# Row tiles 0 and 1 of a fused prologue in smaller parts, row tile 1's transposes later

## The chip, the cores and the metric

The kernel runs on one core of one Trainium2 chip. The metric is the device time of one execution in microseconds (us). A profile's span, from the first to the last instruction of the profiled execution, is about 1.8 us shorter than that execution's time.

## The reference, cut to what matters

The program normalises x (2048 x 640), runs attention over the last 512 cached positions on it with 32 heads, and multiplies the result with a gate that comes from a SwiGLU network on the same normalised x. Only the start of the network matters here: the first product that needs the normalised x.

```
xn = _layernorm(x, axis=-1)                  # 2048 x 640
s  = attention(xn, k_cache, v_cache, wq, wo)
h  = _silu(xn @ w_gate) * (xn @ w_up)        # the part at the start of the kernel
g  = _silu(h @ w_down)
return x + s * g
```

## The kernel before

The kernel does the network first. The first 512 rows are four row tiles of 128 rows. For each of them VectorE takes the statistics (two `bn_stats` on 320 columns each, one `bn_aggr`), ScalarE the square root, VectorE the reciprocal and the normalised rows `xn`. PE (TensorE, the matmul engine) transposes `xn` in five chunks of 128 columns into two tiles in PSUM, the memory that it writes its results to, and copies bring the chunks to `xnT`. Then PE multiplies: 30 matmuls for each row tile (five chunks, six PSUM banks: gate and up for three blocks of the hidden dimension). The work of row tile t+1 stands inside the matmuls of row tile t, at matmul 24 of 30:

```python
PARTS = (slice(0, 2), slice(2, NC))          # chunks 0-1, chunks 2-4
...
def ready(t):
    xn, rows = xns.pop(t), slice(t * P, (t + 1) * P)
    for tp, cs in zip(tps, PARTS):           # five transposes, two PSUM tiles
        for k, c in enumerate(range(cs.start, cs.stop)):
            nc.tensor.transpose(tp[:, k, :], xn[:, c * P : (c + 1) * P], ident[:])
    for tp, cs in zip(tps, PARTS):           # two copies
        part = tp[:, 0 : cs.stop - cs.start, :]
        if t == 3 and cs.stop == NC:
            nc.vector.tensor_copy(out=xnT[:, cs, rows], in_=part)
        else:
            nc.scalar.copy(xnT[:, cs, rows], part)
...
for k, (f, s, cs) in enumerate(order):
    if k == len(order) * 4 // 5 and t < 3:   # 24 of 30
        ...                                  # ln_apply(t + 1), and statistics of a later tile
        ready(t + 1)
        ...
    hidden_mm(first[f][s][:, rows], s, f, rows, cs)
```

Before all this PE runs 15 matmuls on zeros (`keep_warm`), while x and the weights are being loaded.

The softmax here doesn't subtract the row's maximum and nothing guards it: scores larger than these inputs give would overflow.

## Time and profile before

| | before |
|---|---|
| time, median of the first 3 runs | 922.87 us (922.42 to 922.88) |
| span of the profile | 920.7 us |
| PE busy | 914.6 us, 99% |
| first matmul of row tile 0, 1, 2, 3 | 6.54, 8.61, 10.68, 12.75 us |
| first matmul on 512 columns, after row tile 3 | 14.47 us |

The views are read thus. A timeline row gives the start, the length, the engine (DVE is VectorE, ACT is ScalarE), the line, the operation, its output and inputs, the shapes and the count; in brackets is the idle time before it and what ended it. Rows of one kind are merged, and their length then runs from the first start to the last end. Matmuls are pipelined: one of 128 columns lasts 0.22 us from start to end, and the next one starts 0.0556 us after it. PE's number of instructions in the page of before is 16 short, as some matmul records are missing from that trace.

### The profile page before, as it was taken

To read this page: it belongs to the slowest core of one execution; us is meant where nothing else is said; L and a number is where in the kernel's file an instruction comes from. 1 tells how busy PE (TensorE), PEld (TensorE's weight loads), DVE (VectorE), ACT (ScalarE), POOL (GpSimd) and SP (SyncE) were. 2 spreads that over 40 slices of the span, in tenths; PEclk is the share of its full clock that TensorE was granted. 3 is DMA by queue.
4 is the path that set the end of the run, shared out by engine and by line. 5 is a ranking of instruction groups with operands and counts; after the bars stand their busy time and mean duration, and the time that the engine had idled before them with its cause. 6 is when DMAs were issued, how large, how long until landed. Compare 5 with 4: busy or idle time off the path is not lost.

```text
span 920.7 us, 25767 instructions
## 1 busy us (share of the span) xinstructions
PE 914.6 (99%) x11086; PEld 625.9 (68%) x11102; DVE 575.8 (63%) x847; ACT 474.6 (52%) x850; POOL 101.9 (11%) x390
## 2 busy tenths in 40 slices
PE   9999999999999999999999999999999999999998
PEld 5455556575858585868686767676777777676666
DVE  6343331467676767676766667676767676767656
ACT  4222222556464646565556565655555555556461
POOL 0000000000000000000000000000000000002978
PEclk9999999999999999999999999999999999999999
DMA  9330510045644444435536262635271717163524
GB/s 308 64 75 18 110 35 1 1 78 89 92 74 85 82 83 83 79 87 70 97 62 104 60 108 53 113 48 119 44 122 36 130 37 126 31 129 86 130 62 142
DMA packets 243762, 77.18 MB, mean 84 GB/s; under 512 B 224576, under 2 KB 243648, under 8 KB 243648
## 3 DMA queue, kind: packets, MB, share of 16 engines
q1 hardware_dynamic: 243216, 75.14, 41.9%
q8 instruction: 87, 1.43, 0.7%
q10 hardware_dynamic: 432, 0.39, 0.2%
q14 instruction: 27, 0.22, 0.1%
HBM read 39.45 MB, written 2.62 MB: 46 GB/s over the span
## 4 chain that ended last, share of the span: by engine, by line
PE 98%; POOL 0%; DMA 0%; DVE 0%; issue 0%; POOLq 0%; ACT 0%; DVEq 0%
PE mm L440 22%; PE sc L576 19%; PE sc L454 18%; PE mm L479 16%; PE sc L277 11%; PE mm L299 6%; PE sc L548 2%; PE mm L531 2%; POOL ob L636 0%; PE gu L277 0%; PE mm L548 0%; PE mm L312 0%; DMA x_t<-in_A_x_dram 0%; PE sc L479 0%; PE sc L531 0%
## 5 line engine op out<-in xcount | busy, mean ns | idle before, releaser
L458 ACT ACTIVATE p_t<-sc 128x1024 bf16<-128x1024 f32 x254 | 253.0, 1023 | 128.2 <-PE sc L454 128.2
L445 DVE TENSOR_REDUCE qT<-mm 128x512 bf16<-128x1024 f32 x189 | 231.1, 1223 | 95.3 <-PE mm L440 92.8
L509 ACT ACTIVATE O_b<-mm,r 128x192 bf16<-128x192 f32 x486 | 165.0, 422 | 180.8 <-issue 156.3
L440 PE MATMUL mm<-xnT,wq_p 64*128 64x512 bf16 x1890 | 240.2, 376 | 0.0
L601 DVE TENSOR_TENSOR sacc<-sacc,sc 128x640 f32<-128x640 f32 x200 | 164.2, 821 | 87.0 <-PE sc L576 87.0
L576 PE MATMUL sc<-wo_p,OT_b 64*128 64x320 bf16 x2592 | 217.3, 296 | 0.0
L454 PE MATMUL sc<-qT,khat 64*128 64x512 bf16 x1524 | 198.2, 376 | 0.0
L479 PE MATMUL mm<-V_p,p_t 64*128 64x193 bf16 x3520 | 186.4, 242 | 0.0
L479 PEld LDWEIGHTS <-p_t 64*128 64x128 bf16 x3584 | 162.9, 93 | 12.1
L440 PEld LDWEIGHTS <-wq_p 64*128 64x128 bf16 x1890 | 105.7, 94 | 93.4 <-issue 0.5
L576 PEld LDWEIGHTS <-OT_b 64*128 64x128 bf16 x2592 | 140.4, 94 | 21.4
L454 PEld LDWEIGHTS <-khat 64*128 64x128 bf16 x1536 | 85.9, 94 | 79.8
L564 POOL MEMSET turn_t<- 128x1 f32 x328 | 32.5, 99 | 691.9 <-PE mm L479 469.7
L285 DVE TENSOR_TENSOR hT<-sc,sg 128x512 bf16<-128x512 f32 x46 | 31.7, 691 | 83.7 <-ACT sg L284 83.7
L284 ACT ACTIVATE sg<-sc 128x512 bf16<-128x512 f32 x46 | 27.3, 597 | 73.4 <-PE sc L277 71.9
L277 PE MATMUL sc<-xnT,wg_sb 128*128 128x512 bf16 (+1 forms) x248 | 59.5, 353 | 0.7
L277 PE MATMUL sc<-xnT,wu_sb 128*128 128x512 bf16 (+1 forms) x259 | 60.2, 354 | 0.1
L299 PE MATMUL mm<-wd_sb,hT 128*128 128x320 bf16 x384 | 56.6, 299 | 0.0
L498 DVE RECIPROCAL r<-mm 128x4 f32<-128x4 f32 x124 | 22.6, 182 | 46.9 <-PE mm L479 36.1
L299 PEld LDWEIGHTS <-hT 128*128 128x128 bf16 x384 | 37.6, 98 | 18.9
L277 PEld LDWEIGHTS <-wu_sb 128*128 128x128 bf16 x285 | 27.1, 98 | 26.9 <-issue 0.2
L277 PEld LDWEIGHTS <-wg_sb 128*128 128x128 bf16 x285 | 27.1, 98 | 22.7
(69 smaller groups left out, 374.9 us busy)
## 6 DMA issues: line engine op xcount, KB each, us to landing
wo_p<-in_A_wo_dram SPq DMA_DIRECT2D x16, 480.0 KB, 4.4
K_p<-in_A_k_cache_dram SPq DMA_DIRECT2D x32, 192.0 KB, 3.3
V_p<-in_A_v_cache_dram SPq DMA_DIRECT2D x32, 192.0 KB, 3.0
wq_p<-in_A_wq_dram SPq DMA_DIRECT2D x64, 80.0 KB, 3.0
wq_p<-in_A_wq_dram SPq DMA_DIRECT2D x16, 160.0 KB, 3.4
x_r<-in_A_x_dram SPq DMA_DIRECT2D x16, 160.0 KB, 4.7
x_t<-in_A_x_dram SPq DMA_DIRECT2D x14, 160.0 KB, 3.0
OT_b<-O_b SPq DMA_TRANSPOSE x124, 3.0
```

The source lines that it names most:

```text
L277: nc.tensor.matmul(out, w_sb[:, c, f * P : (f + 1) * P], xnT[:, c, qc], start=(c == 0), stop=(c == NC - 1),)
L285: nc.vector.tensor_tensor(hTs[b][:, f, :], u, sg[:], ALU.mult)
L299: nc.tensor.matmul(dn[:, 0:HD], hTs[b][:, f, ti * P : (ti + 1) * P], wd_sb[:, f, cols], start=(f == 0), stop=(f == NF - 1),)
L440: nc.tensor.matmul(q_ps[:, h, :], pairs[pr]["wq"][r, c, j * P : (j + 1) * P], xnT[r, c, b * 512 : (b + 1) * 512], start=(c == 0), stop=(c ...
L445: nc.vector.reduce_sum(qTs[i][:, j, :], q_ps[:, :, :].rearrange("p h n -> p n h"), axis=AX.X)
L454: nc.tensor.matmul(sc[:, h, :], khat[r, j, ks], qT[r, j, :], start=(j == 0), stop=(j == 2))
L458: nc.scalar.activation(p_t[:, :, :], sc[:, :, :], ACT.Exp, scale=scale)
L479: m = nc.tensor.matmul(acc[:, k, h * 256 : h * 256 + Dh + 1], Ps[i][kc][r, h, qt * P : (qt + 1) * P], V_p[r, kc, h, 0 : Dh + 1], start=(p ...
L509: nc.scalar.activation(O_b[:, qt, h, :], a_k[:, h, 0:Dh], ACT.Copy, scale=r[:, k, h, :])
L564: st["turn"] = nc.gpsimd.memset(turn_t[:], 0.0)
L576: m = nc.tensor.matmul(ps[:, n, 0:HD], OTs[i][r, 3 * qt + j, :], pairs[i // NB]["wo"][r, j, n * HD : (n + 1) * HD], start=(turn == 0 and j ...
L601: nc.vector.tensor_tensor(s_t, s_t, sc[:, :, 0:HD], ALU.add)
```

## The change

The intent: the first product can start earlier if row tile 0's first chunk is ready sooner (parts of 1, 2 and 2 chunks), and VectorE takes the last copy of row tile 0 so that ScalarE isn't in the way. Row tile 1 is normalised in two parts, and its transposes move behind row tile 0's matmuls: two of them at matmul 28, three after matmul 30.

```diff
-        def ready(t):
-            xn, rows = xns.pop(t), slice(t * P, (t + 1) * P)
-            ...                                   # both parts, as above
+        PARTS = {0: (slice(0, 1), slice(1, 3), slice(3, NC)), 1: (slice(0, 2), slice(2, NC))}
+        COLS = {t: [slice(cs.start * P, cs.stop * P) for cs in parts] for t, parts in PARTS.items()}
+
+        def ready(t, n):
+            cs, rows = PARTS[min(t, 1)][n], slice(t * P, (t + 1) * P)
+            tp = tps[n % 2][:, 0 : cs.stop - cs.start, :]
+            for k, c in enumerate(range(cs.start, cs.stop)):
+                nc.tensor.transpose(tp[:, k, :], xns[t][:, c * P : (c + 1) * P], ident[:])
+            if (t, n) in ((0, 2), (3, 1)):
+                nc.vector.tensor_copy(out=xnT[:, cs, rows], in_=tp)
+            else:
+                nc.scalar.copy(xnT[:, cs, rows], tp)
...
-        ln_stats(1, lambda: ln_apply(0, (slice(0, 2 * P), slice(2 * P, D))))
-        ready(0)
+        ln_stats(1, lambda: ln_apply(0, COLS[0]))
+        for n in range(3):
+            ready(0, n)
...
-                if k == len(order) * 4 // 5 and t < 3:
+                if t == 0 and k == 28:
+                    ln_apply(1, COLS[1])
+                    ready(1, 0)
+                elif t in (1, 2) and k == 24:
...
+            if t == 0:
+                ready(1, 1)
+                ln_stats(2)
+                ln_sqrt(2)
```

More of the change, by code (lines that the diff above doesn't have):

```diff
@@ L215 @@
         psum1 = early.enter_context(tc.tile_pool(name="psum1", bufs=1, space=bass.MemoryType.PSUM))
-        PARTS = (slice(0, 2), slice(2, NC))
         tps = [psum1.tile([P, 8, P], bf, name="tp", tag="tp%d" % n) for n in range(2)]
@@ L318 @@
         hTs[0] = ffh.tile([P, NF, 512], bf, name="hT")
-        def ready(t):
-            xn, rows = xns.pop(t), slice(t * P, (t + 1) * P)
-            for tp, cs in zip(tps, PARTS):
-                for k, c in enumerate(range(cs.start, cs.stop)):
-                    nc.tensor.transpose(tp[:, k, :], xn[:, c * P : (c + 1) * P], ident[:])
-            for tp, cs in zip(tps, PARTS):
-                part = tp[:, 0 : cs.stop - cs.start, :]
-                if t == 3 and cs.stop == NC:
-                    nc.vector.tensor_copy(out=xnT[:, cs, rows], in_=part)
-                else:
-                    nc.scalar.copy(xnT[:, cs, rows], part)
+        PARTS = {0: (slice(0, 1), slice(1, 3), slice(3, NC)), 1: (slice(0, 2), slice(2, NC))}
[9 more added lines that the diff above has]
+                nc.scalar.copy(xnT[:, cs, rows], tp)
         ln_stats(0)
         ln_sqrt(0)
-        ln_stats(1, lambda: ln_apply(0, (slice(0, 2 * P), slice(2 * P, D))))
-        ready(0)
+        ln_stats(1, lambda: ln_apply(0, COLS[0]))
+        for n in range(3):
+            ready(0, n)
         ln_sqrt(1)
@@ L354 @@
                     else:
-                        ln_apply(t + 1)
-                    ready(t + 1)
-                    if t == 0:
-                        ln_stats(2)
-                    if t < 2:
-                        ln_sqrt(t + 2)
+                        ln_apply(3)
+                    for n in range(2):
+                        ready(t + 1, n)
+                    if t == 1:
+                        ln_sqrt(3)
                     else:
```

## The prediction

> **What bounds the kernel now.** I read the page first, then the view of waits of the PE, then the timelines of PE, ScalarE and VectorE between 3.5 and 14 us. On the page, the busy line and the chain that ended last:
>
> ```profile
> PE 914.6 (99%) x11086; PEld 625.9 (68%) x11102; DVE 575.8 (63%) x847; ACT 474.6 (52%) x850; POOL 101.9 (11%) x390
> ...
> PE 98%; POOL 0%; DMA 0%; DVE 0%; issue 0%; POOLq 0%; ACT 0%; DVEq 0%
> ```
>
> TensorE sets the end from start to finish. The view of waits for PE has two rows only, both in the first 6 us:
>
> ```profile
> PE gu L225 <- DVE zero_t L174: 1.2, 1, 1.2
> PE tp L326 <- DVE xn L262: 0.2, 1, 0.2
> ```
>
> The stage table says the same: 332.00 us busy of 332.00 between 168 and 500 us, 27.04 of 27.20 between 12.8 and 40 us. After about 13 us nothing can absorb a delay of PE and nothing can profit from an idle engine, so the change is worth exactly what it does to the moment when PE starts on row tile 3, and no more. The change touches only the prologue, where row tiles 0 to 3 are normalised (VectorE), transposed (PE, L326), copied from PSUM (ScalarE, L332) and multiplied (PE, L277).
>
> The timeline there, in which the PE rows give issue times 0.055 us apart and each row's own length overlaps the next:
>
> ```profile
> 5.39 0.64 DVE L262 TENSOR_SCALAR xn<-x_t,mv,rstd 128x256 bf16<-128x256 bf16 x2
> 5.79 0.63 PE L326 MATMUL tp<-ident,xn 128*128 128x128 bf16 x5 [0.19 <-DVE xn L262]
> 6.11 0.82 ACT L332 COPY xnT<-tp 128x256 bf16<-128x256 bf16 x2 [0.96 <-PE tp L326]
> 6.54 0.22 PE L277 MATMUL sc<-xnT,wg_sb 128*128 128x128 bf16 x1
> ...
> 7.88 0.44 PE L326 MATMUL tp<-ident,xn 128*128 128x128 bf16 x5
> 8.19 0.75 ACT L332 COPY xnT<-tp 128x256 bf16<-128x256 bf16 x2 [1.05 <-PE tp L326]
> 8.43 0.22 PE L277 MATMUL gu<-xnT,wu_sb 128*128 128x128 bf16 x1
> 8.61 0.22 PE L277 MATMUL sc<-xnT,wg_sb 128*128 128x128 bf16 x1
> ```
>
> From the first transpose (5.79) to the first matmul of row tile 3 (12.75 in the same view) are 6.96 us; the 20 transposes and 90 matmuls between need 110 x 0.0556 = 6.12. So 0.84 us are holes: 0.18 inside row tile 0's transposes (the third waits for the second part of xn), 0.29 before its first matmul (6.25 to 6.54), and 0.12 before the first matmul of each of row tiles 1, 2 and 3 (8.49 to 8.61, for example). That 0.84 is all there is to win.
>
> A transpose-to-matmul latency follows: row tile 1's first transpose is at 7.88, its copy starts at 8.19 and its first matmul at 8.61, that is 0.73 us. Row tiles 2 and 3 show the same (9.95 to 10.68, 12.02 to 12.75). In that time the kernel has 5 transposes and 6 matmuls to issue, 11 x 0.0556 = 0.61; the missing 0.12 is the hole.
>
> The VectorE timeline is nearly full in this stage:
>
> ```profile
> 6.46 0.21 DVE L241 BATCH_NORM_AGGREGATE mv<-stats 128x2 f32<-128x12 f32 x1
> 7.16 0.16 DVE L260 RECIPROCAL rstd<-rstd 128x1 f32<-128x1 f32 x1 [0.49 <-ACT rstd L251]
> 7.36 0.45 DVE L262 TENSOR_SCALAR xn<-x_t,mv,rstd 128x640 bf16<-128x640 bf16 x1
> 7.72 0.88 DVE L238 BATCH_NORM_STATS2 stats<-x_t 128x6 f32<-128x320 bf16 x2
> 8.63 0.21 DVE L241 BATCH_NORM_AGGREGATE mv<-stats 128x2 f32<-128x12 f32 x1
> 8.76 0.44 DVE L238 BATCH_NORM_STATS2 stats<-x_t 128x6 f32<-128x320 bf16 x1
> 9.21 0.16 DVE L260 RECIPROCAL rstd<-rstd 128x1 f32<-128x1 f32 x1
> 9.40 0.45 DVE L262 TENSOR_SCALAR xn<-x_t,mv,rstd 128x640 bf16<-128x640 bf16 x1
> ```
>
> Row tile 2's xn ends at 9.85; with the 0.05 that a hand-over to PE takes (5.74 to 5.79 for row tile 0) it is ready at 9.90, and PE transposes it at 9.95. So VectorE is only 0.05 us ahead of PE there. From 7.36 to 9.40 it runs without a break.
>
> **What the Trainium skill says.** "TensorE: Matmul & The Clock Gate", Part 2 (Step-by-step): weight loads may be pulled ahead, but "The MATMULs themselves stay in program order". The trace agrees: the transposes and L277 appear in program order, and a stuck transpose holds what follows. The same page (Single matmul latency, Back-to-back issue gap) gives (398 + N)/2.4 = 219 ns and about 56 ns for N = 128; the trace has 219 ns and 0.0556 us. "ScalarE: Activation LUTs", What ACT_TABLE_LOAD costs, gives 0.833 ns per element and a fixed part; the trace's copies take 372 ns for 256 columns and 484 for 384, so 0.875 ns per column, and I use those: 260 ns for 128 columns. "Perfetto Trace Analysis", Optimizing Scalar/DVE Operations: VectorE pays a fixed overhead per instruction (some 60 ns on SBUF, and about twice that in the profile), yet breaking an instruction up may let work finish sooner where it causes bubbles. The trace has a larger price: TENSOR_SCALAR on 256, 384 and 640 columns takes 346, 373 and 446 ns, and the next start follows after 0.26, 0.29 and 0.36 us, so nearly 0.2 us of each is fixed.
>
> **The change part by part.** The order of instructions that the compiler leaves: PE issues all five transposes of row tile 0 (1, 2, 2) before the first matmul, and the third pair waits for ScalarE's copy of part 0, because it reuses its PSUM tile. Row tile 1's transposes move from position 24 of row tile 0's 30 matmuls to position 28 (two chunks), then 2 matmuls, then three chunks.
>
> *Row tile 0.* xn by parts: 128 columns at 5.39, length about 0.32 (346 less 27 for 128 columns), the next starts at 5.62, the third at 5.88. First transpose 5.76; ends 5.99; copy of part 0 at 6.02, ends 6.28. Part 1: xn ends 5.97, transposes 6.02 and 6.08, copy 6.33 to 6.70. Part 2: xn ends 6.23, the PSUM tile is free at 6.28 + 0.06 = 6.34, transposes 6.34 and 6.40. First matmul 6.45, against 6.54: **0.09 us won**. Chunk 1 is needed at 6.45 + 6 x 0.0556 = 6.79 and is there at 6.76. VectorE's copy of part 2 comes behind bn_stats and bn_aggr at about 6.8, ends near 7.1, and is needed at 6.45 + 15 x 0.0556 = 7.28: no wait.
>
> *Row tile 1.* VectorE: the three pieces cost 0.23 + 0.26 + 0.26 = 0.75 against 0.55, so bn_stats starts at 6.14 in place of 5.94; bn_aggr ends 6.87. Before, the square root was held back by ScalarE's copies to 6.83; now it starts at 6.90, so 0.07 later. Reciprocal 7.23, xn part 0 at 7.43, ready for PE at 7.83. PE comes to position 28 at 6.45 + 1.56 = 8.01, so xn isn't waited for; part 1 (7.69 to 8.07) is there too. But from 8.01 the first matmul of row tile 1 still needs the latency of 0.73, so 8.74, and PE has only 2 transposes, 2 matmuls and 3 transposes to put in between: 7 x 0.0556 = 0.39. The hole grows from 0.12 to 0.34. Row tile 1 starts at 8.74 against 8.61: the 0.09 has become **0.13 lost**.
>
> *Row tile 2.* xn of row tile 1 in two parts costs VectorE 0.26 + 0.29 = 0.55 against 0.36, so 0.19; with the 0.07 all that follows is about 0.27 later: row tile 2's xn at 9.67 to 10.12, ready 10.17. PE arrives at its transposes at 8.74 + 24 x 0.0556 = 10.07, so it now waits 0.10. The transposes start 10.17 against 9.95: **0.22 lost**. Code from here on is unchanged: first matmul of row tile 2 at 10.90.
>
> *Row tile 3.* The square root waits for ScalarE's copies, which are 0.22 later with the transposes; xn ready at about 12.16, PE arrives at 12.23: no new wait. First matmul 12.97 against 12.75. The sum is +0.22 us, and it goes through to the end: 922.87 + 0.22 = 923.1.
>
> **The rivals.** First, a gain: the author's intent. If row tile 1's first copy began before 8.1 us, or row tile 2's xn came in time, the 0.09 would stay, and one of the holes could close: 922.5 to 922.8. For it: the earlier first matmul is solid. Against it: the 0.73 latency appears three times alike, and 7 slots can't cover it. Second, VectorE as the bound: if a piece costs more than I read, or its PSUM copy delays the reciprocal, row tiles 2 and 3 both wait for xn and the loss is 0.3 to 0.5: 923.2 to 923.4. For it: the slack of 0.05 before. Against it: bn_aggr's square root gives the copy 0.3 us of idle VectorE to hide in. Third, weights: an earlier first matmul might wait for a DMA. The loads of the first two chunks are issued at 0.72 and 1.23 and take 3.4 and 4.0 us, so they land by 5.3, and those of the rest (1.74 and 2.24, 4.3 and 4.8 us) by 7.1, needed at 7.1 and 7.6. Close for one, but hidden: 0 to 0.1.
>
> **Range and chances.** The whole stage that is touched holds 0.84 us of holes, and no path adds over 1 us; 2% would be 18 us. So neither side of 2% is reachable by this change, and only a disturbed run could show it. The effect I expect, 0.22, is less than the spread of the three runs before (922.42 to 922.88, 0.46). The range is the effect of -0.3 to +0.5 with that spread: 922.4 to 923.6. Faster 0.01, same 0.98, slower 0.01.
>
> **What would show it.** Right: first L277 matmul near 6.45; row tile 1's first transpose near 8.01; a hole of about 0.3 before row tile 1's first matmul (8.74); PE waiting about 0.1 for VectorE's xn at 10.1; first matmul of row tile 3 near 12.97; everything after shifted by the same amount. Wrong: a first matmul after 6.54 (the PSUM reuse costs more), no hole before row tile 1, no wait for xn at row tile 2, or a start of row tile 3 at or before 12.75. Any difference that arises after 14 us would mean that I missed a coupling.

## The result, and the profile after

| | before | after |
|---|---|---|
| time, median of 6 runs each | 922.69 us (922.42 to 922.88) | 922.95 us (922.62 to 923.37) |
| ratio | | 1.0003, 95% interval 0.999 to 1.0016 |
| span of the profile | 920.7 us | 920.9 us |
| first matmul of row tile 0, 1, 2, 3 | 6.54, 8.61, 10.68, 12.75 us | 6.49, 8.79, 10.89, 12.96 us |
| first matmul on 512 columns | 14.47 us | 14.67 us |

A ratio here is the mean time of one kernel's fast runs over that of the other's of the same rounds, so it isn't quite the ratio of the medians. The page after, busy times and the chain that ended last:

```profile
PE 915.7 (99%) x11102; PEld 626.1 (68%) x11102; DVE 576.5 (63%) x850; ACT 474.5 (52%) x850; POOL 101.9 (11%) x390
...
PE 99%; POOL 0%; issue 0%; DVE 0%; POOLq 0%; ACT 0%; DVEq 0%
```

PE still sets the end. VectorE has three instructions more (850 for 847): one more piece of row tile 0, one more of row tile 1, one copy. ScalarE has the same number, as it gained a small copy and gave one away. The view of waits of PE lists:

```profile
PE gu L224 <- DVE zero_t L174: 1.2, 1, 1.2
PE sc L276 <- ACT xnT L332: 0.2, 1, 0.2
```

A wait for ScalarE's copy (L332) is new in the list. That the wait for `xn` of row tile 0 has gone is not the change's doing: in this profile the last warming matmuls took 0.31 us each and their lengths cover it; in the second profile of the same kernel (after_again, below) it is listed again with 0.2 us. PE's timeline shows the new wait, at row tile 1:

```profile
8.00 0.22 PE L276 MATMUL sc<-xnT,wu_sb 128*128 128x128 bf16 x1
8.06 0.28 PE L328 MATMUL tp<-ident,xn 128*128 128x128 bf16 x2
8.17 0.22 PE L276 MATMUL sc<-xnT,wu_sb 128*128 128x128 bf16 x1
8.22 0.22 PE L276 MATMUL gu<-xnT,wu_sb 128*128 128x128 bf16 x1
8.28 0.33 PE L328 MATMUL tp<-ident,xn 128*128 128x128 bf16 x3
8.79 0.22 PE L276 MATMUL sc<-xnT,wg_sb 128*128 128x128 bf16 x1 [0.18 <-ACT xnT L332]
```

From the first transpose (8.06) to the first matmul of row tile 1 (8.79) are 0.73 us, as before. But only seven instructions are issued in that time, the first transpose among them, so PE has issued the last of them at 8.39 and waits to 8.79 for its turn; in issue time the hole is 8.79 - 8.45 = 0.34 us. The brackets show 0.18, because the pipelined lengths run on to 8.61. VectorE's timeline, row tile 1 and 2:

```profile
7.20 0.16 DVE L259 RECIPROCAL rstd<-rstd 128x1 f32<-128x1 f32 x1
7.40 0.64 DVE L261 TENSOR_SCALAR xn<-x_t,mv,rstd 128x256 bf16<-128x256 bf16 x2
7.96 0.88 DVE L237 BATCH_NORM_STATS2 stats<-x_t 128x6 f32<-128x320 bf16 x2
8.87 0.21 DVE L240 BATCH_NORM_AGGREGATE mv<-stats 128x2 f32<-128x12 f32 x1
8.99 0.44 DVE L237 BATCH_NORM_STATS2 stats<-x_t 128x6 f32<-128x320 bf16 x1
9.44 0.16 DVE L259 RECIPROCAL rstd<-rstd 128x1 f32<-128x1 f32 x1
9.64 0.45 DVE L261 TENSOR_SCALAR xn<-x_t,mv,rstd 128x640 bf16<-128x640 bf16 x1
```

The reciprocal comes 0.04 us later than before (7.16 there), the next `bn_stats` 0.24 later (7.72 there), and row tile 2's `xn` 0.24 later (9.40 there).

**Where the 0.2 us is.** It arises before the first 512-column matmul, and nowhere else. The span from that matmul to the end is 920.7 - 14.47 = 906.23 us before and 920.9 - 14.67 = 906.23 after. Over all twelve profiles it lies between 906.17 and 906.34. So the prologue can be compared alone, and far more sharply than the times can. As x arrives a little earlier or later from run to run (VectorE's first `bn_stats` starts between 3.52 and 3.95 us), the experiments are measured from that `bn_stats`. That gives, for the first 512-column matmul, 10.77 us before (14.47 - 3.70) and 10.99 after (14.67 - 3.68): a loss of 0.22.

### The profile page after: what moved, and what is told of

Its sections match the earlier page's. It is cut to its first block, busy times and chain, and to the rows that moved or that the text cites. A ratio compares the mean times of both kernels' runs of the same rounds, so it can differ in the third digit from the quotient of the medians.

```text
span 920.9 us, 25788 instructions
## 1 busy us (share of the span) xinstructions
PE 915.7 (99%) x11102; PEld 626.1 (68%) x11102; DVE 576.5 (63%) x850; ACT 474.5 (52%) x850; POOL 101.9 (11%) x390
## 4 chain that ended last, share of the span: by engine, by line
PE 99%; POOL 0%; issue 0%; DVE 0%; POOLq 0%; ACT 0%; DVEq 0%
PE mm L447 22%; PE sc L583 19%; PE sc L461 18%; PE mm L486 16%; PE sc L276 11%; PE mm L298 6%; PE sc L555 2%; PE mm L538 2%; PE gu L224 1%; POOL ob L643 0%; PE gu L276 0%; PE mm L555 0%; PE mm L311 0%; PE sc L538 0%; PE sc L486 0%
```

## The experiments

All kernels gave correct results. All numbers in the table are us from VectorE's first `bn_stats`, out of the timelines of PE and VectorE, except for the last two columns: the median time, and that of before in the same rounds. "Slow clock" is explained under the table; in after the clock came up only during the transposes, in the others before the first one or at it.

| kernel | row tile 0 | 1 | 2 | 3 | first 512 | time | before |
|---|---|---|---|---|---|---|---|
| before | 2.84 | 4.91 | 6.98 | 9.05 | 10.77 | | |
| before_again (slow clock) | 2.94 | 5.22 | 7.29 | 9.37 | 11.08 | 922.63 | 922.70 |
| after (clock up in the transposes) | 2.81 | 5.11 | 7.21 | 9.28 | 10.99 | 922.95 | 922.69 |
| after_again | 2.76 | 5.05 | 7.22 | 9.29 | 11.00 | 922.92 | 922.70 |
| rt0_parts_only | 2.76 | 4.98 | 7.05 | 9.12 | 10.84 | 922.50 | 922.70 |
| rt1_parts_only | 2.84 | 5.14 | 7.21 | 9.28 | 10.99 | 922.65 | 922.70 |
| pos24_two_pieces | 2.76 | 4.88 | 7.21 | 9.28 | 11.00 | 922.86 | 922.51 |
| pos28_one_piece | 2.75 | 5.05 | 7.12 | 9.19 | 10.91 | 922.77 | 922.51 |
| earlier_transposes | 2.84 | 4.92 | 6.96 | 8.93 | 10.72 | 922.49 | 922.51 |
| earlier_stats | 2.84 | 4.92 | 6.88 | 8.84 | 10.63 | 922.59 | 922.51 |
| earlier_stats_pairs (slow clock) | 2.95 | 5.14 | 7.11 | 9.06 | 10.74 | 922.50 | 922.54 |
| earlier_stats_pairs_again | 2.85 | 4.99 | 6.95 | 8.91 | 10.59 | 922.22 | 922.59 |

Every ratio's interval contains 1, so the times decide none of these; the profiles do.

**The two kernels again, unchanged.**

> The kernel before, unchanged, as a second profile and a null for the times. Measured from VectorE's first bn_stats, the first matmul of row tiles 0, 1, 2, 3 came at 2.84, 4.91, 6.98, 9.05 us in the first profile. If these are set by the order of instructions alone, this run repeats them within 0.03 us, and the time within 0.3 us of its partner. If the clock of the PE array at the start (how long the warming matmuls run slow) moves them, they differ by 0.05 us or more between two profiles of the same kernel, and the loss of 0.23 us in the changed kernel would be in doubt.

> The changed kernel, unchanged, a second profile. From the first bn_stats: 2.81, 5.11, 7.21, 9.28 us for the first matmul of row tiles 0 to 3 in its first profile, so 0.23 us later than before at row tile 3. In that profile the last warming matmuls and the first transpose were still slow (the first transpose 0.29 us against 0.23). If the clock was unlucky, row tile 0 comes 0.04 to 0.07 earlier now (2.74 to 2.77) and all later tiles with it; the loss at row tile 3 would be 0.16 to 0.23. Time 0.2 to 0.3 us longer than its partner.

The changed kernel repeated itself within 0.01 us at row tile 3, this time with the clock up before the first transpose. Row tiles 0 and 1 came 0.05 and 0.06 earlier than in its first profile, as expected; row tiles 2 and 3 did not, against the expectation, because PE then stood 0.07 us before row tile 2's transposes (9.86 to 9.99 us, less one issue), until VectorE's `xn` was there:

```profile
9.86 0.22 PE L276 MATMUL gu<-xnT,wu_sb 128*128 128x128 bf16 x1
9.99 0.45 PE L328 MATMUL tp<-ident,xn 128*128 128x128 bf16 x5
```

The kernel before did not repeat itself: it came 0.32 us later at row tile 3. Its PE timeline:

```profile
5.47 0.42 PE L225 MATMUL gu<-zero_t 128*128 128x128 bf16 x2
5.79 0.79 PE L326 MATMUL tp<-ident,xn 128*128 128x128 bf16 x5
6.64 0.27 PE L277 MATMUL sc<-xnT,wg_sb 128*128 128x128 bf16 x1
6.70 0.31 PE L277 MATMUL sc<-xnT,wu_sb 128*128 128x128 bf16 x1
6.81 0.31 PE L277 MATMUL sc<-xnT,wg_sb 128*128 128x128 bf16 x1
6.92 0.31 PE L277 MATMUL sc<-xnT,wu_sb 128*128 128x128 bf16 x1
```

These matmuls take 0.31 us for 0.22 and follow one another after 0.11 us in place of 0.0556. The Trainium skill, "TensorE: Matmul & The Clock Gate", Part 1 (The HAM clock gate), says that the array starts at half its clock, is released after a window of activity of some 3.4 us, and that the window runs freely, so that the moment differs from run to run. The trace agrees in the spacing (0.11 us against the page's 107 ns at half clock). In this profile the release came only after row tile 0's first matmuls; in the first profile of before it came before the transposes (the warming matmuls follow one another after 0.06 us from 5.21 us on). The clock that the windows view reports stood at 1.00 in both, so it doesn't show this; the durations do. The late clock cost 0.10 us up to the first matmul and 0.21 more up to row tile 1's; from there on the two profiles of before make the same steps (2.07, 2.08 and 1.71 us, against 2.07, 2.07 and 1.72). For the comparison it means that only profiles with the same clock at the transposes may be set side by side, and I could compare the two slow ones (11.08 and 10.74) only with each other. By this rule the pair for the change is before and after_again: 10.77 and 11.00, a loss of 0.23; before with an early clock was profiled once. The changed kernel was never profiled with a clock as late as in before_again, so its loss there is not shown.

**One half of the change at a time.**

```diff
# rt0_parts_only, against the changed kernel
-                if t == 0 and k == 28:
-                    ln_apply(1, COLS[1])
-                    ready(1, 0)
+                if t == 0 and k == 24:
+                    ln_apply(1)
+                    for n in range(2):
+                        ready(1, n)
+                    ln_stats(2)
+                    ln_sqrt(2)
...
-            if t == 0:
-                ready(1, 1)
-                ln_stats(2)
-                ln_sqrt(2)
```

> Row tile 0 in three parts, row tile 1 as before (one normalisation, five transposes at matmul 24). My theory (the loss is made at row tile 1, by its transposes at position 28): row tile 0 at 2.78 to 2.81, row tile 1 at 4.95, row tile 2 at 7.01, row tile 3 at 9.08, so a loss of 0.03 and no gain, because VectorE's xn of row tile 1 sets row tile 1. Rival (VectorE's three pieces and its PSUM copy make the loss): row tile 3 at 9.2 or later.

```diff
# rt1_parts_only, against the changed kernel
-        PARTS = {0: (slice(0, 1), slice(1, 3), slice(3, NC)), 1: ...}
+        PARTS = {0: (slice(0, 2), slice(2, NC)), 1: ...}
-            if (t, n) in ((0, 2), (3, 1)):
+            if (t, n) == (3, 1):
-        for n in range(3):
+        for n in range(2):
             ready(0, n)
```

> Row tile 0 as before, row tile 1 in two parts at matmul 28 and 30. My theory: row tile 0 at 2.84, row tile 1 at 5.13, row tile 2 at 7.19, row tile 3 at 9.26, the whole loss of about 0.21 us with this part alone, and no wait for xn before row tile 2's transposes. Rival (VectorE's work for row tile 0 makes the loss): row tile 3 at 9.05 to 9.10.

Row tile 1's half alone makes the whole loss (first 512 at 10.99, as with both), all of it in the hole before row tile 1 (5.14 for 4.91), and PE doesn't wait for `xn` before row tile 2, as expected. Row tile 0's half alone wins 0.08 us at its own first matmul and has lost 0.07 by row tile 1, a little more than the 0.03 that I had expected; its row tile 3, at 9.12, lies between my 9.08 and the rival's 9.2. Its timeline shows why nothing is left of the win:

```profile
7.68 0.22 PE L276 MATMUL gu<-xnT,wu_sb 128*128 128x128 bf16 x1
7.87 0.45 PE L328 MATMUL tp<-ident,xn 128*128 128x128 bf16 x5
```

PE comes to row tile 1's transposes 0.13 us too soon (7.74, one issue after 7.68) and stands until VectorE has delivered `xn`, which with three pieces for row tile 0 comes 0.07 us later after the first `bn_stats` than before (3.73 for 3.66). The PE that starts earlier has nothing to do earlier.

**Position and pieces.** Row tile 1's half has two parts again: where its transposes stand (24 or 28), and whether VectorE writes `xn` in one piece or two. With row tile 0 in three parts, four combinations were run; they aren't quite a square, as pos24_two_pieces moves two of the five transposes back to 24 and leaves three behind 30, while rt0_parts_only has all five at 24.

```diff
# pos24_two_pieces, against the changed kernel
-                if t == 0 and k == 28:
+                if t == 0 and k == 24:
# pos28_one_piece, against the changed kernel
-                    ln_apply(1, COLS[1])
+                    ln_apply(1)
```

> The changed kernel with row tile 1's first two transposes back at matmul 24 (its other three stay behind matmul 30). All from VectorE's first bn_stats, for a profile with the clock up before the first transpose. Theory (two limits of nearly the same length, the latency from transposes to matmuls and VectorE's chain): the hole before row tile 1 shrinks to 0.12, so row tile 1 at 4.86 in place of 5.05; but VectorE hasn't become faster, so PE now waits about 0.25 us for xn before row tile 2's transposes, and row tile 2 comes at 7.20, row tile 3 at 9.26: the loss stays at about 0.21. Rival (position 28 alone is the cause): row tile 1 at 4.86, no wait for xn, row tile 3 at 9.0 to 9.07.

> The changed kernel with row tile 1 normalised by one instruction again (its transposes and copies stay in two parts at matmul 28 and 30). Theory: row tile 1 at 5.05 as in the changed kernel (latency), VectorE 0.19 earlier afterwards, so no wait for xn before row tile 2; row tile 2 at 7.12, row tile 3 at 9.18: loss 0.13 in place of 0.23. Rival (VectorE's pieces don't matter): row tile 3 stays at 9.28. Other rival (VectorE's pieces are all of it): row tile 3 at 9.05.

| first 512, against 10.77 of before | `xn` in one piece | `xn` in two pieces |
|---|---|---|
| transposes at 24 | +0.07 (rt0_parts_only) | +0.23 (pos24_two_pieces) |
| transposes at 28 | +0.14 (pos28_one_piece) | +0.22, +0.23 (after, after_again) |

Row tile 0's three parts are in every cell, +0.07 by themselves. Beside that the position alone costs 0.07 more and the two pieces alone 0.16 more, and both together cost no more than the two pieces do. In pos24_two_pieces the hole before row tile 1 is back to its old size (row tile 1 at 4.88), and PE waits one step later instead:

```profile
9.92 0.22 PE L276 MATMUL gu<-xnT,wu_sb 128*128 128x128 bf16 x1
10.22 0.45 PE L328 MATMUL tp<-ident,xn 128*128 128x128 bf16 x5
```

The gap from 9.92 to 10.22 is one issue (0.06) and a wait of 0.24 us for row tile 2's `xn`, which VectorE wrote at 9.72 to 10.17. The three transposes left behind matmul 30 don't set this: VectorE ran without a break from row tile 1's first piece (7.49) to row tile 2's reciprocal (9.52), and the square root that the reciprocal needs was done at 9.49. So two limits of almost the same length stand beside each other: PE's latency from transposes to matmuls, and VectorE's chain. The rival "the position alone" has fallen (row tile 3 at 9.28, not 9.07), and so has "the pieces alone" (9.19 with one piece, not 9.05; 0.07 of that is row tile 0's half, which has 9.12 by itself).

**A version that starts row tile 3 sooner.** If this holds, it helps to put the transposes earlier and to shorten VectorE's chain. All three kernels start from the kernel before.

```diff
# earlier_transposes, against the kernel before
-                if k == len(order) * 4 // 5 and t < 3:
+                if k == 22 and t < 3:
...                 # for t == 1: ln_sqrt(3) is issued between the two copies of ready(2)
# earlier_stats, in addition
+        load_x(2)                        # was two lines further down
         load_first(slice(2, NC))
...
         ready(0)
         ln_sqrt(1)
+        st2 = [ln_stats_halves(2)]       # first bn_stats of row tile 2, in VectorE's idle time
...                 # its second bn_stats, bn_aggr and ln_sqrt(2) between the two copies of ready(1)
# earlier_stats_pairs, in addition
-                order = [(*fs, range(NC)) for fs in banks]
+                order = [(f, s, [c]) for f in range(3) for c in range(NC) for s in range(2)]
...
-                if t == 3 and s == 1:
+                if t == 3 and s == 1 and NC - 1 in cs:
```

> The kernel before with the transposes of row tiles 1 to 3 at matmul 22 in place of 24 (two more matmuls to cover the latency) and the square root of row tile 3 put between ScalarE's two copies of row tile 2. Theory: row tile 1 at 4.89 (PE waits for xn), row tile 2 at 6.93 (waits for xn), row tile 3 at 8.88 without a hole, so 0.17 us won over before's 9.05. Rival (the hole returns elsewhere, as ScalarE's second copy is later): row tile 3 at 9.05 or later. In the time 0.2 us is near the noise; 922.5.

> As earlier_transposes, and VectorE's chain shortened: x of row tile 2 is loaded before the weights of chunks 2 to 4, the first bn_stats of row tile 2 runs in VectorE's idle time before row tile 1's reciprocal, and its square root stands between ScalarE's two copies of row tile 1. Theory: row tile 1 at 4.89, row tile 2 at 6.84, row tile 3 at 8.79, holes only before row tile 1: 0.26 us won. Rival: the weights of chunks 2 to 4 land about 0.4 us later and PE waits for them in row tile 0, up to 0.2, so nothing is won. Time 922.3 to 922.5 if the theory holds.

Both went the expected way at row tile 3's first matmul (8.93 and 8.84, expected 8.88 and 8.79), but at the first 512-column matmul only 0.05 and 0.14 us were left of 0.12 and 0.21. PE's timeline of earlier_transposes, row tile 3's first two groups of five matmuls:

```profile
12.61 0.56 PE L277 MATMUL sc<-xnT,wg_sb 128*128 128x128 bf16 x5
13.00 0.44 PE L277 MATMUL sc<-xnT,wu_sb 128*128 128x128 bf16 x5
```

The first group takes 0.39 us to the next (12.61 to 13.00) where five matmuls need 0.28; before took 0.33 (12.75 to 13.08). In this row tile the order is bank by bank, so chunk 2 is wanted 0.11 us after the first matmul, and VectorE's copy of chunks 2 to 4 (12.42 to 12.78 in its timeline) isn't done. Hence the third kernel.

> As earlier_stats, and row tile 3's matmuls in another order: for each pair of gate and up bank, chunk by chunk, so that chunk 2 is needed after 4 matmuls in place of 2. In earlier_stats row tile 3's first group took 0.08 us longer than elsewhere, waiting for VectorE's copy of chunks 2 to 4. Measure: the first matmul on 512 columns after row tile 3, from VectorE's first bn_stats: 10.77 before, 11.00 in the changed kernel, 10.63 in earlier_stats. Theory: 10.55, with the clock up before the first transpose; the rest of the span from there stays at 906.2. Rival: another copy or the SiLU table is waited for, and it stays at 10.63. In the time 0.2 us under before, which five rounds may not resolve beside the spread of about 1 us.

> The same kernel as earlier_stats_pairs, because its profile fell on a start with slow transposes and slow first matmuls (10.74 us from the first bn_stats to the first 512-column matmul, the clock up only at about 7.1 us). If the clock comes up before the first transpose this time: 10.55. If it is late again: 10.7 to 10.8, to be compared with 11.08 of the second profile of before, which had the same late clock.

The first profile of this kernel fell on a late clock (10.74, against 11.08 of before with a late clock); the second one, with the clock up at the first transpose, gave 10.59, so 0.18 us less than before. That it missed 10.55 has a reason that the rival of earlier_stats had named, a late load of weights. In row tile 0 PE stood 0.17 us (7.60 to 7.83, less one issue) for the up weights of chunks 2 to 4, and row tile 1 came at 4.99 in place of 4.92. The view of waits lists it for the weight loads (PEld), not for PE:

```profile
7.60 0.22 PE L288 MATMUL gu<-xnT,wg_sb 128*128 128x128 bf16 x1
7.83 0.23 PE L288 MATMUL sc<-xnT,wu_sb 128*128 128x128 bf16 x1
...
PEld L288 <- DMA wu_sb<-in_B_w_up_dram: 0.2, 1, 0.2
```

So moving the load of row tile 2's x forward is not free: in earlier_stats, where x came 0.31 us later (first `bn_stats` at 3.95), the wait didn't show.

In the second set of times its median was 922.22 us against 922.59 (ratio 0.9995, interval 0.9981 to 1.0008); in the first one 922.50 against 922.54. So it beats both kernels in the profile; the times of the second set lean the same way and don't prove it.

## Why the prediction was right or wrong

The prediction said 923.1 us, +0.22 on 922.87. Measured was 922.95; the median of before moved to 922.69 with more runs, so the medians differ by +0.26, but the interval of the ratio contains 1 and the times alone don't show a direction. The profiles do: +0.22 at the first 512-column matmul, or +0.23 with the clock early in both. The mechanism was right; that the sum fits to 0.01 us owes something to luck, as errors in two steps cancelled. By its steps:

- **Row tile 0.** Predicted 0.09 us won. In the first profile after it was 0.05 (6.49 for 6.54), or 0.03 from the first `bn_stats`; in the second one 0.08. The term that was mis-sized in the first is the first transpose's length: predicted 0.23 (5.76 to 5.99), measured 0.29 with the clock still low, and 0.23 in the second profile. The prediction named no clock.
- **Row tile 1.** Predicted 0.13 lost, from a latency of 0.73 with seven issues to cover it. Measured: 0.73 again, seven issues, a hole of 0.34, as predicted; the loss from the first `bn_stats` was 0.20 in the first profile and 0.14 in the second (5.11 and 5.05 for 4.91). rt1_parts_only and the hole's bracket show the cause.
- **Row tile 2.** Predicted a wait of 0.10 for `xn` and 0.22 lost. The wait was about 0.01 in the first profile (10.07 to 10.14 with one issue of 0.06) and 0.07 in the second, because row tile 1 came later than predicted in the first; `xn` itself came 0.24 later than before, for a predicted 0.27. The two errors cancel in the first profile, since whichever limit is later decides: 0.23 lost, and 0.24 in the second.
- **Row tile 3 and the end.** Predicted no new wait and +0.22. Measured 12.96 for 12.97, no wait before the transposes (12.17 to 12.22, one issue), and the rest of the span unchanged at 906.2 us. That a shift goes through to the end is confirmed by all twelve profiles.
- **The rivals.** The gain fell. VectorE as the bound was half right: its copy from PSUM hid in idle time, as predicted, but pos24_two_pieces shows that row tile 1's pieces, on top of row tile 0's, would have brought the whole 0.23 us without the move to 28. The weights were no wait in the changed kernel.

What remains open is whether the loss can be seen in the time alone. The mean of after is above that of before in both sets (by about 0.3 us), but a spread of 1.4 us within the five runs of after_again (922.51 to 923.87), and of 1.6 us in earlier_transposes, covers it. The start of the clock can be a part of that spread: two profiles of the kernel before differ by 0.31 us through it. What makes the rest is open, as no slower run was profiled. Open too is the change's effect when the clock comes up late.

## What to carry to other kernels

When two engines hand row tiles to each other and both chains are within a few hundredths of a microsecond of the same length, splitting work on one of them may only move the wait, as it did here: ask first how many issues stand between a transpose and its first use, and how far ahead the engine that feeds it is. Every split here cost the fixed part of an instruction on the engine that does it (about 0.2 us on VectorE), and an earlier start is worth something only if the next tile's input is earlier too. For differences this small, compare the moment at which the touched stage ends in the profile, check that the rest of the span is equal, and check that the array's clock was in the same state.

## What the Trainium skill lacked or had wrong

- "TensorE: Matmul & The Clock Gate", Back-to-back issue gap, gives some 81 ns for each matmul of 128 columns in a stream where every matmul has its own weight load, and 56 ns for the isolated gap. Here 24 such pairs took 8.61 to 9.95 us, so 56 ns each, with a weight load before each.
- "Perfetto Trace Analysis", Optimizing Scalar/DVE Operations, has some 60 ns of fixed engine time for VectorE on SBUF. TENSOR_SCALAR with two per-row operands started its successor after 0.23 us on 128 columns and 0.36 on 640, so the fixed part was about 0.2 us.
- No page has the latency that decided this case, from a PE transpose over a ScalarE copy of 256 columns to the first matmul on it: 0.73 to 0.75 us for row tiles 1 to 3 in all twelve profiles.
- "TensorE: Matmul & The Clock Gate", Part 1, was right that the release of the clock differs from run to run: in the twelve profiles PE's spacing shortened between 4.9 and 7.1 us, 3.7 to 5.9 us after the first warming matmul. What that costs at the start of this kernel, 0.31 us between two profiles, is more than the change did.
